# First 1024 tokens started in two token halves, with new loads, conv reads and a split last block

## The chip, the cores and the metric

The kernel runs on one core of one Trainium2 chip. The metric is device time in microseconds (us) of one execution, as the median of several runs. The core's engines run side by side, each in the order of its own program, and wait for each other through semaphores: TensorE (PE in the profile; PEld is its weight load), VectorE (DVE), ScalarE (ACT), GpSimd (POOL), and SyncE (SP), which here only issues DMAs. ACT and POOL issue DMAs as well.

## The reference

```python
def _attn_ref(x, weight):              # x (8, 4096, 192), weight (8, 7)
    w = softmax(weight, axis=-1)       # one set of 7 taps for each of 8 heads
    x_pad = concat([zeros(8, 6, 192), x], axis=1)
    # head h owns channels 24h .. 24h+23
    out[b, s, h, :] = sum_k w[h, k] * x_pad[b, s + k, h, :]
def _moe_ref(x, w_in, w_out):          # w_in (192, 2048), w_out (2048, 192)
    h = x @ w_in
    g = where(h > 0, h, exp(min(h, 0)) - 1)
    return g @ w_out
```

The softmax is written short here; the reference subtracts the maximum and adds 1e-9 to the sum. 32768 tokens go through a causal 7-tap convolution along the sequence and then through the two products with an ELU between.

## The kernel before, in words

**Tiling.** The tokens are cut into 32 "supers" of 1024 tokens; a super is two groups g (or r) of 512. The feed-forward width of 2048 is cut into 16 slices q of 128. A step n is one pair (super, q). In each step each group has one unit: three matmuls "h" (L993) of 64 rows by 512 tokens, one for each third j of the 192 channels, which sum into one PSUM bank. Group 0 uses rows 0 to 63 of the array and group 1 rows 64 to 127, so two streams of matmuls run side by side; the code calls a stream `rt`. w_in lies in both row halves.

**ELU.** Each unit goes through three engines: ACT takes exp out of PSUM into E (L739), POOL clamps it to at most 1 (L692), DVE writes gT = max(E - 1, h) as fp16 (L855). Only then is the unit's PSUM bank free. There are eight banks.

**Second product.** Matmuls "o" (L1016) take gT of 128 tokens and w_out of one q into an accumulator for (k, g), where k counts half supers of 256 tokens per group. Each accumulator is evacuated (L746, the last one by DVE at L846) and sent out (L544).

**Convolution.** For supers 1 to 31 it is a product with a band matrix `Tm` ("c", L968): windows of 112 tokens, stationary 64 (and 54) rows by 112 columns, 240 moving columns of xg, 16 matmuls a super. ACT evacuates into csb (L735) and a transposing DMA puts it into `att`. `Tm` is made through a band written to DRAM and read back (L1039, L1048). The channels are split as 24h + 8j + e, so a read of one third j of a head takes 8 neighbouring elements at a time.

**The first super** has no such time, and is done another way: x is loaded whole by ACT's queue (L704), cast in three pieces (L714), transposed on PE (L916; L927 for the 8 tokens ahead of group 1), evacuated (L811 on DVE, L726 on ACT), convolved on PE with seven diagonal matrices `taps` (made by one instruction, L791), and evacuated into `att` (L730, L838, L840). Of thirds 0 and 1, two of the seven taps are computed on DVE (L820, L825: `ON_DVE`). Before this, PE runs ten matmuls on zeros (L890, `WARM`), six ahead of the broadcast of the softmaxed taps (L894, L901) and four after it.

**What sets the order.** A planner in plain Python writes the order of every engine before the launch. `live` plays the first 16 steps against a small model of the engines (durations such as `MM_H`, `MM_O`, `MM_C` and expected landings `LANDS`), `block_items` and `emit` the rest; the result is sorted by time into `pe_order`, `act_order` and `dve_order`. At run time each engine follows its list and waits.

**DMA queues.** POOL issues, in this order: w_in in three column parts of three DMAs each (L628), the first of three parts of w_out (L639), x of super 1 (two DMAs, L608), the other parts of w_out, x of super 2; then it begins with the clamps. w_in lands in rows 0 to 63; its copy for rows 64 to 127 is made by ACT (L720), DVE (L843) and a DMA of SP (L1056).

Of the kernel before, what the change touches and what calls it, by code (L numbers as in the profile page):

```python
# [37 lines left out]
WARM = (6, 1, 4)  # L38
WCOLS = ((0, 4 * FC), (4 * FC, 8 * FC), (8 * FC, 16 * FC))
WOUT = (0, 4, 8, 16)  # L40
HALO = 8
BW = P
ON_DVE = (2, 2, 0)
XL = GS - CW * (NWIN - 1) + PAD
XI = SUP // P
# [7 lines left out]
LATE_Q, COPY_AT = 10, 6  # L53
LIVE, UNTIL = 16, 16
EARLY_O = (4, 8)
LANDS = {"x": {1: 7200.0, 2: 14200.0}, "w_in": 10200.0, "w_out": (3900.0, 8400.0, 11000.0)}
# [3 lines left out]
TURNS = 260.0  # L60
X_AT = ((2, 1, 1), (1, 1, 0))
ZERO_AT = 8
# [3 lines left out]
def bass_lightweight_conv__then__act_elu_kernel(  # L66
# [21 lines left out]
    NK = 2 * NS  # L88
# [12 lines left out]
    conv_half = {}  # L101

# [15 lines left out]
    def modelled():  # L118
        return step[0] < UNTIL
# [9 lines left out]

    def h_items(n, r):  # L130
        def issue(j):
            take_bank(("h", n, r), r)
            plan.append((clock[r], ("h", n, r, j)))
            if j == 2:
                freed[bank_of["h", n, r]] = clock[r] + MM_H + HELD["h"]
                if modelled():
                    elu(n, r, clock[r] + MM_H)

        return [(MM_H, lambda j=j: issue(j), None) for j in range(3)]
# [15 lines left out]
    def o_items(k, g, rt, qs, visit, first, final):  # L155


        todo = [(q, kb) for q in qs for kb in range(2)]

        def issue(i):  # L160
            q, kb = todo[i]
            take_bank(("a", k, g), rt)
            if modelled():
                t = NQ * (k // 2) + q
                clock[rt] = max(clock[rt], gt_at[t, g], turned.get((k, g), 0.0) if first and i == 0 else 0.0)
            starts, ends = first and i == 0, final and i == len(todo) - 1
            item = ("o", k, g, rt, q, kb, visit if starts else None, ends)
            plan.append((clock[rt] - AHEAD, item))
            if ends:
                visits[k, g] = visit + 1  # L170
                turned[k, g] = clock[rt] + MM_O + TURNS
# [36 lines left out]
    def block_items(n, g, rt):  # L208
        k, b = divmod(n - O_AT[g], NB)
        if k < 1:  # L210
            q = n - EARLY_O[g]
            if not 0 <= q < NQ:
                return []
            items = o_items(0, g, rt, range(q, q + 1), 2 * q + rt, True, True)
            return evacuated(items, 0, g) if q == NQ - 1 and rt == 1 else items
# [3 lines left out]
    def live(last, convs, turns):  # L219
        hq = [list(range(last)) for _ in range(2)]  # L220
        cq = [list(convs), list(convs)]
        far = float("inf")

        def h_ready(rt):
# [8 lines left out]
            late = rt == 1 and s == 0 and q >= LATE_Q  # L233
            return max(min(freed), att_at[s], LANDS["w_in"] if late else 0.0)
# [11 lines left out]
        def o_ready(rt, g):  # L246
# [5 lines left out]
            t = max(gt_at.get((NQ * (k // 2) + q, g), far) for q in range(q0, q1))  # L252
# [6 lines left out]
        while any(hq) or any(cq) or any(map(any, turns)):  # L259
            best = None  # L260
            for rt in range(2):
# [22 lines left out]
            if what[0] == "h":  # L284
                n = hq[rt].pop(0)
                go(h_items(n, rt))
            elif what[0] == "c":
# [7 lines left out]
            else:  # L295
                g = what[1]
                k, q0, q1, visit = turns[rt][g].pop(0)
                go(o_items(k, g, rt, range(q0, q1), visit, True, True))
# [9 lines left out]
    start_up = [("t", j) for j in (0, 3, 1, 2)] + [("d", j) for j in range(3)]  # L308
    for i, (b, what) in enumerate(
        ((0, ("t", 0)), (3, ("t", 3)), (1, ("t", 1)), (2, ("t", 2)))  # L310
        + ((4, ("d", 0)), (5, ("d", 1)), (6, ("d", 2)), (7, ("d", 2)))
    ):
        occupant[b], freed[b] = what, i - 10.0
        bank_of.setdefault(what, b)
    turns = [[[], []], [[], []]]
    for rt in range(2):
        for g in range(2):
            turns[rt][g] += [(0, q, q + 1, 2 * q + rt) for q in range(LIVE - EARLY_O[g])]
    live(LIVE, [(n, m) for n in range(LIVE) for m in conv_steps.get(n, ())], turns)
    for n in range(LIVE, NP):  # L320
        step[0] = n
        if n == UNTIL:
            clock[:] = [max(clock)] * 2
# [11 lines left out]
    for second in range(2):  # L335
        for rt in range(2):
# [3 lines left out]
            if second == 0:  # L340
                lead = TAIL - (late - QB * b)
                for kk, q0, q1, v, first in (
                    (k, QB * b, late, 2 * b, True),
                    (k + 1, 0, lead, 0, True),
                    (k, late, NQ, 2 * b, False),
                    (k + 1, lead, NQ, 0, False),
                ):
                    tail[rt] += o_items(kk, g, rt, range(q0, q1), v, first, not first)
            else:
                for kk, q0, v in ((k, QB * b, 2 * b), (k + 1, 0, 0)):  # L350
# [4 lines left out]
    pe_order += [("w", 0, WARM[0]), ("s",), ("w", 0, WARM[2])]  # L355
    for what in start_up:
        pe_order.append(what)
# [3 lines left out]
    for at, item in sorted(plan, key=lambda p: p[0]):  # L361
        if item[0] == "h" and item[3] == 2:
# [3 lines left out]
            act_order.append(item[:3])  # L366
        elif item[0] == "c" and item[2:] == (1, HU - 1):
# [18 lines left out]
    x_before = {}  # L386
    for s in range(2, NS):
# [11 lines left out]
    with ExitStack() as stack:  # L399
# [15 lines left out]
        xs = sbuf("xs", [P, XI, D], FP32)  # L415
        xh = sbuf("xh", [HALO, D], FP32)
        xbh = sbuf("xbh", [HALO, 3, 2, HP], BF16)
        xb = sbuf("xb", [P, 3, XI, HP], BF16)
# [16 lines left out]
        part = sbuf("part", [P, 2, GS], FP32)  # L435
# [10 lines left out]
        s_w = [sema(f"s_w{i}") for i in range(6)]  # L446
        s_wc = sema("s_wc")
        s_sel = sema("s_sel")
# [5 lines left out]
        s_xs = sema("s_xs")  # L454
# [17 lines left out]
        s_wd = sema("s_wd")  # L472
        s_wa = sema("s_wa")
        s_band = sema("s_band")
        s_part = sema("s_part")
# [35 lines left out]
        def att_need(s):  # L511
# [4 lines left out]
            ("t", 0): (0, 1),  # L516
            ("t", 1): (1, 0),
            ("t", 2): (2, 0),
            ("t", 3): (0, 2),
            ("d", 0): (0, 3),  # L520
            ("d", 1): (0, 4),
            ("d", 2): (3, 5),
# [7 lines left out]
        def transposed(j):  # L530
            if j == 3:
                return xT[:, :, 0:HALO], H[:, bank_of["t", 3], 0 : 3 * HALO].rearrange(
                    "p (j c) -> p j c", j=3
                )
            return xT[:, j, HALO : HALO + GS], H[:, bank_of["t", j], :]

        def first_att(j, c0, c1):
            b = bank_of["d", j] + (j == 2 and c0 > 0)
            return att[:, 0, j, c0:c1], H[:, b, c0:c1]

        def out_group(eng, k, g):
            t, half = divmod(k, 2)
            row = SUP * t + GS * g + 2 * P * half
            eng.dma_start(  # L544
                out[row : row + 2 * P, :].rearrange("(k p) d -> p k d", p=P),
                osb[:, k % 2, g, :, :],
            ).then_inc(s_out[k % 2], 16)
# [25 lines left out]
        def out_evac(W, k, g):  # L573
            W(s_out[k % 2], 32 * (k // 2))
            W(s_fin[g], k + 1)
            return (
                osb[:, k % 2, g, :, :].rearrange("p k d -> p (k d)"),
                acc_of(k, g)[:, 0 : 2 * D],
# [14 lines left out]
        def _gpsimd(g: bass.BassGpSimd):  # L593
# [31 lines left out]
            def load_w_in(k):  # L625
                c0, c1 = WCOLS[k]
                for j in range(3):
                    g.dma_start(  # L628
                        w_in[0:HP, j, c0:c1],
                        bass.AP(  # L630
                            tensor=moe_w_in.tensor,
                            offset=8 * j * FF + c0,
                            ap=[[CPH * FF, HEADS], [FF, 8], [1, c1 - c0]],
                        ),
                    ).then_inc(s_w[k], 16)

            def load_w_out(k):
# [3 lines left out]
                ).then_inc(s_w[3 + k], 16)  # L641
# [11 lines left out]
            ).then_inc(s_id)  # L653
            for step in range(2):
# [20 lines left out]
            load_w_in(0)  # L675
            load_w_in(1)
            load_w_in(2)
            load_w_out(0)
            for gr in range(2):
                load_x(1, gr)  # L680
            load_w_out(1)
            load_w_out(2)
            for gr in range(2):
                load_x(2, gr)
# [17 lines left out]
        def _scalar(a):  # L702
            W = Waits(a)
            a.dma_start(  # L704
                xs[:, :, :], x_flat[0:SUP, :].rearrange("(p i) d -> p i d", i=XI)
            ).then_inc(s_xs, 16)
# [5 lines left out]
            W(s_xs, 16)  # L712
            for j in range(3):
                a.activation(  # L714
                    xb[:, j, :, :].rearrange("p i (h e) -> p (i h) e", e=8),
                    xs[:, :, :].rearrange("p i (h j e) -> p j (i h) e", j=3, e=8)[:, j],
                    ACT.Copy,
                ).then_inc(s_cast)
            def upper_half(c0, c1):
                a.activation(  # L720
                    w_in[HP:P, :, c0:c1], w_in[0:HP, :, c0:c1], ACT.Copy
                ).then_inc(s_wa)

            for j in range(1, 3):
                W(s_xt, j + 2)
                a.activation(*transposed(j), ACT.Copy).then_inc(s_fa)  # L726
            W(s_w[0], 48)
            upper_half(*WCOLS[0])
            W(s_first, 3)
            a.activation(*first_att(2, 0, GS // 2), ACT.Copy).then_inc(s_fa)  # L730
            for item in act_order:
                if item[0] == "c":
# [3 lines left out]
                elif item[0] == "h":  # L736
# [5 lines left out]
                    if i == COPY_AT:  # L742
                        W(s_w[2], 48)
                        upper_half(WCOLS[2][0], FC * LATE_Q)
# [6 lines left out]
        def _vector(v):  # L751
            W = Waits(v)

# [33 lines left out]
            ).then_inc(s_set)  # L787
            W(s_sel, 1)
            v.tensor_copy(wcol[:], H[:, bank_of["d", 2], 0:KSIZE]).then_inc(s_tap)
            W(s_tap, 1)  # L790
            v.tensor_tensor(  # L791
                taps[:],
                ident[:, :].unsqueeze(1).to_broadcast([P, KSIZE, P]),
                wcol[:, :].unsqueeze(2).to_broadcast([P, KSIZE, P]),
                ALU.mult,
            ).then_inc(s_tap)
            W(s_xh, 16)
            W(s_xz, 1)
            v.tensor_copy(
# [298 lines left out]
```

## Time and profile before

| | us |
|---|---|
| median of 3 runs (723.69 to 724.35) | 723.8 |
| the profiled execution, whole | 723.52 |
| its span in the profile | 721.7 |
| x landed, first cast begins (L714) | 5.45 |
| first conv matmul of super 0 (L944) | 8.09 |
| first h matmul (L993) | 11.68 |
| first exp (L739) / clamp (L692) / gT (L855) | 12.76 / 13.47 / 14.20 |
| last evacuation begins (L846) | 718.31 |

Times in the profile count from the start of the span. In a row of the timeline the first two numbers are start and duration, "x24" is the number of instructions merged into the row, and a name such as "H<-att,w_in" is the output and its inputs (H is PSUM). What follows "<-" in brackets is what ended the engine's idle time. PE's matmuls are pipelined: a duration in a row includes the way through the array, and what one matmul costs in a dense stream is the distance between starts.

### The profile page before, as it was taken

The page shows a single profiled execution, that of the slowest core. Times are in us where ns is not written, and L with a number is a line of the kernel's source. Part 1 is how long each engine was busy: PE and PEld are TensorE (multiplying, and loading weights), DVE is VectorE, ACT ScalarE, POOL GpSimd, SP SyncE. Part 2 cuts the span into 40 slices and gives each one's busy share as a digit, 9 for nine tenths or more (in the row PEclk, how much of TensorE's full clock was granted, in tenths as well). Part 3 has the DMA queues.
Part 4 walks back from the last instruction along what each step waited for, and adds up shares of the span by engine and source line. Part 5 has one row for each costly group of instructions (what it writes and reads, how often), then busy time and mean ns, then how long its engine had stood idle before and what let it go on. Part 6 is the DMA issues. An engine that isn't in the chain of part 4 may idle for free.

```text
span 721.7 us, 27608 instructions
## 1 busy us (share of the span) xinstructions
PE 715.8 (99%) x11846; PEld 677.6 (94%) x11847; DVE 642.7 (89%) x1048; ACT 677.9 (94%) x1287; POOL 670.0 (93%) x1115
## 2 busy tenths in 40 slices
PE   8999999999999999999999999999999999999998
PEld 4689999999999999999999999999999999999997
DVE  7988898998899988989888989988989989999994
ACT  6999999999999999999999999999999999999994
POOL 9999999999999999999999999999999999999893
PEclk9999999999999999999999999999999999999999
DMA  9655353554254663344553555652535543644212
GB/s 171 92 87 75 67 91 74 95 87 82 54 96 72 87 97 61 75 84 85 87 97 50 84 74 96 86 85 51 96 73 90 92 69 66 94 77 83 71 35 68
DMA packets 132703, 58.75 MB, mean 81 GB/s; under 512 B 98582, under 2 KB 132004, under 8 KB 132580
## 3 DMA queue, kind: packets, MB, share of 16 engines
q1 hardware_dynamic: 88228, 39.23, 23.8%
q0 software_dynamic: 43936, 16.77, 22.8%
q8 instruction: 93, 1.52, 0.8%
q10 hardware_dynamic: 416, 0.98, 0.4%
q14 instruction: 30, 0.25, 0.2%
HBM read 34.63 MB, written 25.46 MB: 83 GB/s over the span
## 4 chain that ended last, share of the span: by engine, by line
PE 95%; POOL 2%; DVE 1%; ACT 1%; issue 0%; DVEq 0%; POOLq 0%
PE H L1016 54%; PE H L993 38%; PE H L968 3%; DVE gT L855 1%; POOL w_in L628 1%; ACT E L739 1%; POOL xg L608 0%; POOL w_out L639 0%; ACT csb L735 0%; POOL E L692 0%; POOL owner L656 0%; DVE osb L846 0%; ACT osb L746 0%; POOL block L666 0%; POOL ident L645 0%
## 5 line engine op out<-in xcount | busy, mean ns | idle before, releaser
L855 DVE SCALAR_TENSOR_TENSOR gT<-E,H 128x512 f16<-128x512 f32 x1024 | 632.8, 681 | 65.0 <-POOL E L692 63.2
L1016 PE MATMUL H<-w_out,gT 64*128 64x192 f16 x8192 | 681.9, 243 | 0.1
L993 PE MATMUL H<-att,w_in 64*128 64x512 bf16 x3072 | 680.0, 376 | 0.5 <-DVE gT L855 0.3
L1016 PEld LDWEIGHTS H<-w_out,gT 64*128 64x128 f16 x8192 | 624.0, 94 | 22.9 <-PE H L1016 1.8
L692 POOL TENSOR_SCALAR E<-E 128x512 f32<-128x512 f32 x1024 | 607.6, 614 | 39.3 <-ACT E L739 28.6
L739 ACT ACTIVATE E<-H 128x512 f32<-128x512 f32 x1024 | 592.7, 601 | 27.3 <-PE H L993 1.6
L993 PEld LDWEIGHTS H<-att,w_in 64*128 64x128 bf16 x3072 | 275.4, 93 | 7.8 <-issue 1.2
L968 PE MATMUL H<-xg,Tm 64*112 64x240 bf16 x496 | 92.5, 266 | 0.1
L735 ACT ACTIVATE csb<-H 112x480 bf16<-112x480 f32 x124 | 70.0, 565 | 0.3 <-PE H L968 0.2
L746 ACT ACTIVATE osb<-H 128x384 f32<-128x384 f32 x127 | 61.6, 486 | 7.5 <-PE H L1016 7.4
L968 PEld LDWEIGHTS H<-xg,Tm 64*112 64x112 bf16 x496 | 57.5, 125 | 3.3 <-DVE gT L855 1.1
L608 POOL DMA_DIRECT2D xg<-in_x_dram x62 | 55.3, 893 | 0.2 <-issue 0.2
L846 DVE COPY osb<-H 128x384 f32<-128x384 f32 x1 | 0.6, 556 | 7.3 <-PE H L1016 7.3
L890 PE MATMUL H<-zw 128*128 128x512 bf16 x10 | 4.4, 606 | 1.2 <-DVE zw L754 1.2
L628 POOL DMA_DIRECT2D w_in<-in_moe_w_in_dram x9 | 5.2, 617 | 0.0
L890 PEld LDWEIGHTS H<-zw 128*128 128x128 bf16 x10 | 1.1, 133 | 3.0 <-issue 1.7
L714 ACT ACTIVATE xb<-xs 128x512 bf16<-128x512 f32 x3 | 1.7, 618 | 2.4 <-DMA xs<-in_x_dram 2.4
L944 PE MATMUL H<-xT,taps 128*128 128x256 bf16 (+1 forms) x23 | 3.7, 314 | 0.2 <-issue 0.2
L944 PEld LDWEIGHTS H<-xT,taps 128*128 128x128 bf16 x24 | 2.2, 97 | 1.5
L639 POOL DMA_DIRECT2D w_out<-in_moe_w_out_dram x3 | 2.6, 879 | 0.0
L707 ACT ACT_TABLE_LOAD x1 | 1.3, 1283 | 1.2 <-PEq L1083 1.2
L720 ACT ACTIVATE w_in<-w_in 64x1536 bf16<-64x1536 bf16 (+1 forms) x2 | 2.3, 1162 | 0.0
(43 smaller groups left out, 19.7 us busy)
## 6 DMA issues: line engine op xcount, KB each, us to landing
out_dram<-osb SPq DMA_DIRECT2D x127, 192.0 KB, 3.4
xg<-in_x_dram POOLq DMA_DIRECT2D x61, 240.0 KB, 5.0
xs<-in_x_dram ACTq DMA_DIRECT2D x1, 768.0 KB, 4.6
att<-csb SPq DMA_TRANSPOSE x31, 4.3
w_in<-in_moe_w_in_dram POOLq DMA_DIRECT2D x6, 64.0 KB, 2.9
w_in<-in_moe_w_in_dram POOLq DMA_DIRECT2D x3, 128.0 KB, 5.2
w_out<-in_moe_w_out_dram POOLq DMA_DIRECT2D x2, 192.0 KB, 9.0
w_out<-in_moe_w_out_dram POOLq DMA_DIRECT2D x1, 384.0 KB, 11.7
```

Of the source, the lines that this page charges most:

```text
L608: g.dma_start(xg[0:rows, b, 2 * w0 + gr : 2 * w1 : 2, :], src).then_inc(s_x[b][gr], 16)
L628: g.dma_start(w_in[0:HP, j, c0:c1], bass.AP(tensor=moe_w_in.tensor, offset=8 * j * FF + c0, ap=[[CPH * FF, HEADS], [FF, 8], [1, c1 - c0]], ...
L692: g.tensor_scalar(out=E[:, i % NE, :], in0=E[:, i % NE, :], scalar1=1.0, scalar2=0.0, op0=ALU.min, op1=ALU.max,).then_inc(s_clp)
L735: a.activation(*conv_evac(W, m), ACT.Copy).then_inc(s_ce)
L739: a.activation(E[:, i % NE, :], H[:, bank_of[item], :], ACT.Exp).then_inc(s_exp)
L746: a.activation(*out_evac(W, *item[1:]), ACT.Copy).then_inc(s_oev[item[2]])
L855: v.scalar_tensor_tensor(out=gT[:, s % NG3, q, u, :], in0=E[:, i % NE, :], scalar=1.0, in1=H[:, bank_of[item], :], op0=ALU.subtract, op1=A ...
L890: pe.matmul(H[:, bank, :], zw[:, 0:P], zw[:, 0:GS], start=True, stop=True)
L944: ins = pe.matmul(H[:, bank_of[item] + half, c0:c1], taps[:, tap, :], xT[:, j, HALO - PAD + tap + c0 : HALO - PAD + tap + c1], start=(tap ...
L968: ins = pe.matmul(H[0:CW, bank_of["c", m], 256 * q : 256 * q + UC], Tm[rows, h, 0:CW], xg[rows, s % NXB, :, CPH * h : CPH * (h + 1)].rearr ...
L993: ins = pe.matmul(H[:, bank_of[item[:3]], :], w_in[HP * r : HP * (r + 1), j, FC * q : FC * (q + 1)], att[HP * r : HP * (r + 1), s % 2, j, ...
L1016: ins = pe.matmul(acc_of(k, g)[:, D * kb : D * (kb + 1)], gT[HP * rt : HP * (rt + 1), t % NG3, q, g, t0 : t0 + P], w_out[HP * rt : HP * (r ...
```

## The change

The first super is worked in two halves of 256 tokens per group (`GH` = 256).

- ACT's queue issues the 8 halo tokens (before: SP's) and x in two DMAs, one for each half. The cast is one instruction a half.
- Transposes "t" and convolution "d" of half 0 come first; the transposes "T" of half 1 follow directly. The convolution "D" of half 1 stands in the planner's list: 7 taps of third 0, then of 1, after two steps of h, and of third 2 after three (`JOBS`). All 21 taps run on PE; DVE's part is gone. The evacuations go to ACT (d 0, d 2, D 0 and 1 together, D 2) and DVE (d 1, T).
- The first four steps are two q's each on half 0 (q 0 to 7, six matmuls of 256 columns), the next four the same on half 1 (`SPLIT`). Then steps are whole again.
- `taps` is made by seven instructions; the transposed halo is evacuated among them. Only one matmul on zeros comes after the broadcast, not four.
- w_in is loaded in four DMAs of 512 columns (before: nine), the first ahead of `owner` and `block8` on POOL. The order is then w_in 1 to 3, w_out 0 and 1, x of super 1, w_out 2; x of super 2 is issued ahead of the first clamp, as before.
- The upper rows of w_in are copied by DVE (parts 0 and 1), ACT (q 8 and 9) and SP's DMA.
- Channels are split as 3c + j: conv matmuls read every third element of xg. Their stationary is all 128 columns of `Tm`, not 112.
- The accumulators of the last half super are split into two of 128 tokens, so there is one evacuation and one store more per group, each half as large.

```diff
-WARM = (6, 1, 4)
-WCOLS = ((0, 4 * FC), (4 * FC, 8 * FC), (8 * FC, 16 * FC))
+WARM = (6, 1, 1)
+NCH = 4
+LATE_Q, COPY_AT = 10, 8
+SPLIT = 8
-ON_DVE = (2, 2, 0)
+JOBS = ((2, ("D", 0, 0)), (2, ("D", 0, 1)), (3, ("D", 1, 2)))
-    NK = 2 * NS
+    NK = 2 * NS + 1
...
-    start_up = [("t", j) for j in (0, 3, 1, 2)] + [("d", j) for j in range(3)]
+    start_up = [("t", 3), ("w", 0, WARM[2]), ("t", 0), ("t", 1), ("t", 2)]
+    start_up += [("d", j) for j in range(3)] + [("T", 0), ("T", 1)]
...
+            load_w_in(0)
             for step in range(2):
                 W(s_id, 2 + step)
...
-            load_w_in(0)
             load_w_in(1)
             load_w_in(2)
+            load_w_in(3)
             load_w_out(0)
+            load_w_out(1)
             for gr in range(2):
                 load_x(1, gr)
-            load_w_out(1)
             load_w_out(2)
-            for gr in range(2):
-                load_x(2, gr)
...
-            a.dma_start(
-                xs[:, :, :], x_flat[0:SUP, :].rearrange("(p i) d -> p i d", i=XI)
-            ).then_inc(s_xs, 16)
+            a.dma_start(xh[:, :], x_flat[GS - HALO : GS, :]).then_inc(s_xh, 16)
+            for half in range(2):
+                a.dma_start(
+                    xs[:, XI * half : XI * (half + 1), :].rearrange("p i d -> p (i d)"),
...
+            cast(0)
             for j in range(3):
                 W(s_xt, j + 2)
+                a.activation(*first_evac(("t", j)), ACT.Copy).then_inc(s_fa)
+            cast(1)
+            for j in (0, 2):
+                W(s_first, j + 1)
+                a.activation(*first_evac(("d", j)), ACT.Copy).then_inc(s_fa)
...
+            for tap in range(KSIZE):
+                if tap == 1:
+                    W(s_xt, 1)
+                    v.tensor_copy(*first_evac(("t", 3))).then_inc(s_fd)
+                v.tensor_scalar(
+                    out=taps[:, tap, :],
...
+            upper_half(0)
+            W(s_first, 2)
+            v.tensor_copy(*first_evac(("d", 1))).then_inc(s_fd)
             for j in range(2):
+                W(s_xt, 5 + j)
+                v.tensor_copy(*first_evac(("T", j))).then_inc(s_fd)
+            upper_half(1)
...
-                        H[0:CW, bank_of["c", m], 256 * q : 256 * q + UC],
-                        Tm[rows, h, 0:CW],
+                        H[:, bank_of["c", m], 256 * q : 256 * q + UC],
+                        Tm[rows, h, :],
                         xg[rows, s % NXB, :, CPH * h : CPH * (h + 1)].rearrange(
-                            "p w (j i) -> p j w i", j=3
+                            "p w (i j) -> p j w i", j=3
                         ),
```

## The prediction

> **What bounds the kernel now.** I read the shares of the page first, then the chain that ended last, then the timeline of the first 30 us and of the last 7, then single groups. On the page PE is busy all the time, but three others are close behind:
>
> ```profile
> PE 715.8 (99%) x11846; PEld 677.6 (94%) x11847; DVE 642.7 (89%) x1048; ACT 677.9 (94%) x1287; POOL 670.0 (93%) x1115
> ```
>
> The chain tells them apart by stage (start, duration, what):
>
> ```profile
> 2.48 0.73 POOL w_in L628
> 3.22 4.43 POOL w_in L628 x8
> 7.65 0.80 POOL w_out L639
> ...
> 13.51 0.67 POOL E L692
> 14.20 0.70 DVE gT L855
> 15.03 1.92 PE H L993 x9
> ...
> 27.91 6.67 DVE gT L855 x11
> ...
> 64.81 0.25 PE H L993 x2
> ...
> 86.67 0.25 PE H L993 x2
> ```
>
> The reader is to see three stages. Up to 13.5 us a queue of DMA issues on POOL and, beside it, the first super's convolution. Then ELU: DVE alone gives 11 units in 6.67 us, 0.606 us a unit. From about 44 us the same PE rows return every 86.67 - 64.81 = 21.86 us, one super. With the planner's costs, which the starts of the timeline bear out, a stream of PE has 48 h x 0.216 + 128 o x 0.0825 + 8 c x 0.1025 = 21.75 us a super. So the middle is PE, with 0.11 us a super to spare, or 3.1 us over 28 supers.
>
> How much start-up is lost: PE's work over the whole kernel is 1536 x 0.216 + 4096 x 0.0825 + 248 x 0.1025 = 695.1 us a stream. It ends at about 718.2 and begins at 11.68. So 718.2 - 11.7 - 695.1 - 3.1 = 8.3 us are idle after the first h, before 44 us, while units wait for ELU. In that stage PE is not the bound; when ELU starts and how fast it runs sets the time at which PE becomes dense, and all that follows moves with it.
>
> ```profile
> 1.22 1.28 ACT L707 ACT_TABLE_LOAD   x1 [1.22 <-PEq L1083]
> 4.39 1.69 PE L890 MATMUL H<-zw 128*128 128x512 bf16 x4
> 5.45 1.67 ACT L714 ACTIVATE xb<-xs 128x512 bf16<-128x512 f32 x3 [2.40 <-DMA xs<-in_x_dram]
> 8.09 3.65 PE L944 MATMUL H<-xT,taps 128*128 128x512 bf16 x23 [0.16 <-issue]
> 12.76 3.54 ACT L739 ACTIVATE E<-H 128x512 f32<-128x512 f32 x7 [0.60 <-PE H L993]
> 14.20 11.07 DVE L855 SCALAR_TENSOR_TENSOR gT<-E,H 128x512 f16<-128x512 f32 x18 [1.03 <-POOL E L692]
> ```
>
> To be seen in these timeline rows: x is waited for until 5.45; the convolution takes 3.65 us for 10 x 512 + 14 x 256 = 8704 columns, 0.42 ns each; ACT needs 3.54/7 = 0.51 us a unit and DVE 11.07/18 = 0.615, so DVE is the slower once it runs.
>
> **The change, part 1: when ELU starts.** *Taps.* ACT issues three DMAs ahead of its table load, not one: 0.28 (the halo's issue, as it was on SP) + 0.39 = 0.67 us later. The exp of the taps, the small DVE chain and the broadcast move with it: taps' column at 4.49 + 0.67 = 5.16. The halo cast (0.34) fits ahead of it while PE works. Seven tap instructions cost at least the one of now (1.09); with the halo's evacuation (0.17) and a little for each they end at about 6.7, and the band's cast (0.19) at 6.9, before 6.1. *x.* The whole x took 4.6 us from issue to landing. A half is issued at 1.08 and lands between 1.08 + 2.3 = 3.4 and 5.7; I take 4.2. Its cast, 768 elements at the 0.52 us of 512, is 0.8, so done at 5.0. That is hidden: on PE the halo's transpose and one zero matmul (1.69/4 = 0.42) come first, until 5.8. *PE.* 24 transposes at the pace of the 48 now (some 0.03 each) end at 6.6, ACT evacuates the first from 6.25 (0.38, L730's shape) to 6.65. Then 21 matmuls x 256 columns x 0.42 = 2.26 us, so 6.75 to 9.0, then T, 24 x 0.03 = 0.7: the first h at 9.7, against 11.68. Its third j needs the evacuation of d 2, 9.0 + 0.2 + 0.38 = 9.6. ACT's cast of half 1 (0.8) lies behind the evacuations, 7.3 to 8.1, and hides under the convolution. Six h of 0.108 us: the first exp at about 10.6, against 12.76, 2.15 us earlier.
>
> *POOL* must keep up. Nine w_in issues (0.73 + 4.43 = 5.2 us) become four. Bounds: 4 x 0.58 = 2.3 and 4 x 0.9 = 3.6 (issues of xg and w_out, with more pieces each); I take 0.65 each, 2.6. The queue that ends at 13.5 now ends at 10.9, just ahead of the first clamp at 11.2. At 0.9 each it would hold the clamp until 11.9 and cost 0.7. Moving the first w_in ahead delays `block8` to 3.2 us, which is used at 4.6: nothing. *DVE* has its pre-work (two copies of w_in at 0.93, three evacuations) done at 11.6, and starts gT at about 12.1, against 14.20.
>
> **Part 2: what is given back.** The convolution of half 1 costs PE 21 x 0.108 = 2.3 us between steps. It hides in the 8.3 idle us; without them it would cost 2.3. But its evacuations stand in ACT's list between exps: 0.49 + 0.38 = 0.85. DVE is slower than ACT by 0.1 a unit, so part could hide; yet the copy of w_in (0.84, L720) and four evacuations of the next super (0.57 each) follow on ACT within the next units. So of 2.15 I count 0.85 and 0.1 of gaps off: **1.2 us gained**; bounds 2.1 (all hidden) and 0.4 (POOL's 0.7 also lost).
>
> The w_in and w_out loads start up to 2 us earlier on POOL, but the DMA engines are full (in the first 25 us the shares of the 16 engines stand at 8 and 9 tenths), so they land less early, and the band goes out 0.8 later. What is late next is `Tm`, now 8.0 us from issue to landing at about 19.2: PE would stand at super 1's first conv (now at 20.5) for up to 1 us. DVE has some 3 us of units in banks then; cost 0, at worst 1.
>
> **Part 3: the clock of PE.** Six matmuls on zeros take 2.74 us, 0.83 ns a column, and the four later ones run at the same pace; only the convolution runs at 0.42. So PE is at half rate until between 5.6 and 8.1, and the four zero matmuls fill PE from 4.4 to 6.1. The change leaves one, so PE is nearly idle from 3.8 to 5.0. If full rate then came only at about 9.2, some 11 of the 21 matmuls would take 0.213 and not 0.108: 1.15 us. I take nothing, since PE is busy before and after the hole; bounds 0 and 1.15. [...]
>
> **Part 4: the conv of the other 31 supers.**
>
> ```profile
> L968 PEld LDWEIGHTS H<-xg,Tm x40: 122/127/129, 204.0 to 253.9; 64*112 64x112 bf16 x20, 54*112 54x112 bf16 x20
> ```
>
> A load of 112 columns takes 127 ns, one of 128 columns 94 (L1016). The wider one should take 94: 33 ns less, 16 times a super, beside running matmuls; only a load behind a wait is in the open. Bounds: 0, and the whole 0.11 us a super, 3.1. One exposed load a super is 0.9; as a different start can also shift the planned order I take **0.5 us gained**, with -1 at the other end.
>
> The moving read takes every third element, not 8 neighbours. No row shows that. The nearest is the conv itself, whose read jumps after each 8 elements and yet costs 0.1025 us for 240 columns, the same 0.42 ns as a plain row: cost 0. A gain is excluded, as that is already the plain rate. The far end is two reads' time per column, as where PE's transposes write PSUM with a stride (64 columns at some 53 ns, not 27): 0.1 x 248 = 25 us. I take 0, the row being the same instruction. [...]
>
> **Part 5: the tail.**
>
> ```profile
> 718.31 0.56 DVE L846 COPY osb<-H 128x384 f32<-128x384 f32 x1 [7.29 <-PE H L1016]
> 718.90 0.40 ACTq L544 DMA_DIRECT2D out_dram<-osb  x1
> ```
>
> The last evacuation halves. Between 128x256 (0.424, L840) and 128x24 (0.172, L811) a column costs 1.1 ns, so 192 columns less save 0.2. The last store, 2.8 us from issue to the end of the span, carries half the bytes: between 0 and 0.3, I take 0.2. **0.4 us gained.** The added evacuation and store lie earlier, beside PE's last 16 matmuls per stream.
>
> **Sum.** 1.2 + 0.5 + 0.4 = 2.1 us. The profiled execution took 723.52 (span 721.7 and 1.8 around it), so 721.4; the median lies 0.3 above that execution, so **721.7**.
>
> **Rivals.**
> - *Half-rate PE* through the convolution (part 3): 721.7 + 1.15 = 722.9. For it, the hole; against it, busy stretches on both sides. 0.17.
> - *Data come too late*: ELU starts early, but w_out, w_in's upper rows or `Tm` land no earlier, and PE, in order, stands before them. DMA shares near full speak for it, the banks of units ahead of DVE against it. 1.2 us lost: 722.9. This is also the case that the change doesn't do what it says. 0.16.
> - *Slower: the strided conv read.* Place: L968, 248 matmuls a stream. From 2.1/25.4 = 8% per conv matmul on, all gain is gone; at twice the time 721.7 + 25 = 747. For it, that no row shows such a read; against it, the conv row of now. 0.11.
> - Forecast: 0.56.
>
> **How the numbers follow.** About 0.2% (1.45 us, so 722.35 and 725.25) is what can be told from no change. The bounds, taken together, run from 723.8 - (2.1 + 2.0 + 0.5) = 719.2, where part 4 is not counted whole, since its 3.1 would need every idle ns of the middle to be a weight load, to 723.8 - (0.4 - 1 + 0.2) = 724.2. The forecast is faster 8 times in 10, the two cases at 722.9 three in ten: 0.45 + 0.10 = 0.55. Slower: the strided read, and 0.06 from late data with a worse order: 0.17. Same: 0.28. The range goes from 719.2 to 724.5: it takes in these bounds and both cases at 722.9 with their spread, and leaves out the strided read.
>
> **What would show it.** First h near 9.7, first exp near 10.6, first gT near 12.1; D's evacuations between exps; starts of the convolution's matmuls 0.108 apart (0.213: the clock). Dense PE rows from 43 us on, and repeating every 21.84 to 21.86 (22.6 for the strided read). Last evacuation 0.35. Wrong would be: gT starting early, but DVE idle between units by as much; or the period longer.

## The result, and the profile after

The changed kernel takes **760.4 us** (median of 4 runs, 759.84 to 761.15), beside 724.08 for the kernel before on the same chip: 1.050 times as long (95% interval 1.0486 to 1.0518). The forecast of 721.7, with a range of 719.2 to 724.5, was wrong. The profiled execution took 760.21 with a span of 758.3; before it was 721.7, so 36.6 us have to be found. (Two single executions further down, of 1928 and 1065 us where the others of their kernels took 738 to 740 and 723 to 726, are left out of the numbers.)

First the page of the changed kernel, busy time by engine. PE's busy time grew by 16.8 us though it does nearly the same work:

```profile
PE 732.6 (97%) x11910; PEld 677.9 (89%) x11910; DVE 646.4 (85%) x1050; ACT 680.8 (90%) x1291; POOL 669.3 (88%) x1110
```

Then the chain that ended last, in order of time (start, duration, what):

```profile
2.10 27.97 DMA xs<-in_x_dram
30.10 0.85 ACT xb L775
30.99 1.49 PE H L980 x24
32.48 2.67 PE H L1064 x24
...
224.96 0.30 PE H L1064 x2
...
247.26 0.30 PE H L1064 x2
...
269.56 0.30 PE H L1064 x2
...
755.73 0.36 DVE osb L888
```

Two things are to be seen. The chain now begins with a load of x that ends at 30.07; the load of the whole x had ended at 5.45. And the same PE rows return every 22.30 us, no longer every 21.86.

The timeline of the changed kernel's first 40 us shows both halves waited for, and the clock besides:

```profile
1.43 1.19 ACTq L759 DMA_DIRECT2D xs<-in_x_dram  x2
17.71 0.84 ACT L775 ACTIVATE xb<-xs 128x768 bf16<-128x768 f32 x1 [13.23 <-DMA xs<-in_x_dram]
20.03 3.79 PE L1003 MATMUL H<-xT,taps 128*128 128x256 bf16 x21
30.10 0.84 ACT L775 ACTIVATE xb<-xs 128x768 bf16<-128x768 f32 x1 [9.57 <-DMA xs<-in_x_dram]
32.41 2.74 PE L1064 MATMUL H<-att,w_in 64*128 64x256 bf16 x24
35.25 2.55 DVE L904 SCALAR_TENSOR_TENSOR gT<-E,H 128x512 f16<-128x512 f32 x4 [1.41 <-POOL E L745]
```

Half 0 landed at 17.7, 13 us after ACT stood ready for it. The order of PE's list puts T, the transposes of half 1, before the first h, so the first h waits for half 1 as well: 32.41, where it was 11.68. Two windows of that stage (length, busy us of PE, PEld, DVE, ACT and POOL, then granted clock, DMA share, GB/s) show that PE's clock fell too, while PE had little to do:

```profile
17.70:30.10 12.40, 5.21 (x45) 3.88 (x45) 0.43 (x1) 2.00 (x5) 0.00 (x0) 0.84 0.53 111
30.10:32.50 2.40, 1.51 (x26) 1.34 (x28) 0.40 (x1) 1.39 (x3) 0.00 (x0) 0.50 0.20 24
```

Last, the matmuls of the conv in the middle (min/median/max ns), first in the kernel before, then their row and that of their weight loads in the changed kernel:

```profile
L968 PE MATMUL H<-xg,Tm x40: 260/263/307, 204.1 to 254.0; 64*112 64x240 bf16 x20, 54*112 54x240 bf16 x20
```

```profile
L1028 PE MATMUL H<-xg,Tm x45: 325/328/333, 199.8 to 259.9; 64*128 64x240 bf16 x23, 54*128 54x240 bf16 x22
L1028 PEld LDWEIGHTS H<-xg,Tm x44: 92/93/94, 200.3 to 259.7; 54*128 54x128 bf16 x22, 64*128 64x128 bf16 x22
```

The median went from 263 to 328 ns, and two of one stream that follow each other began 0.102 to 0.107 us apart before (one in eight up to 0.147); now 0.162 to 0.170. The weight load did fall from 127 to 93 ns, as forecast. So there are two suspects: **20.7 us** until the first h, and 0.44 us a super, **some 13 to 14 us** over 31 supers. From the start of the last evacuation to the end of the span it is 2.57 us, 0.8 less than before.

### The profile page after: what moved, and what is told of

Same layout as the page of the kernel before. It is cut to its first block, busy times and chain, and to the rows that moved or that the text cites. A ratio compares the mean times of both kernels' runs of the same rounds, so it can differ in the third digit from the quotient of the medians.

```text
span 758.3 us, 27738 instructions
## 1 busy us (share of the span) xinstructions
PE 732.6 (97%) x11910; PEld 677.9 (89%) x11910; DVE 646.4 (85%) x1050; ACT 680.8 (90%) x1291; POOL 669.3 (88%) x1110
## 4 chain that ended last, share of the span: by engine, by line
PE 94%; DMA 4%; ACT 1%; DVE 0%; POOL 0%; ACTq 0%; issue 0%; DVEq 0%
PE H L1087 51%; PE H L1064 38%; PE H L1028 5%; DMA xs<-in_x_dram 4%; PE H L1003 0%; DVE gT L904 0%; ACT E L797 0%; PE H L980 0%; POOL E L745 0%; ACT csb L793 0%; ACT xb L775 0%; ACT w_in L803 0%; ACTq L759 0%; ACTq L757 0%; DVE osb L888 0%
## 5 line engine op out<-in xcount | busy, mean ns | idle before, releaser
L904 DVE SCALAR_TENSOR_TENSOR gT<-E,H 128x512 f16<-128x512 f32 x1024 | 639.2, 683 | 75.4 <-POOL E L745 73.3
L1064 PE MATMUL H<-att,w_in 64*128 64x512 bf16 (+1 forms) x3120 | 681.2, 374 | 0.2 <-ACT csb L793 0.2
L1064 PEld LDWEIGHTS H<-att,w_in 64*128 64x128 bf16 x3120 | 280.3, 94 | 5.1 <-DVE gT L904 1.0
L1028 PE MATMUL H<-xg,Tm 64*128 64x240 bf16 x496 | 122.6, 329 | 0.5 <-DVE gT L904 0.2
L807 ACT ACTIVATE osb<-H 128x384 f32<-128x384 f32 (+1 forms) x129 | 62.1, 483 | 6.8 <-PE H L1087 6.8
L1028 PEld LDWEIGHTS H<-xg,Tm 64*128 64x128 bf16 x496 | 42.1, 93 | 6.1 <-PE H L1028 1.4
L980 PE MATMUL H<-ident,xb 64*64 64x64 bf16 x48 | 3.0, 342 | 19.3 <-ACT xb L775 19.3
L881 DVE CAST att<-H 128x256 bf16<-128x256 f32 x1 | 0.4, 426 | 14.1 <-PE H L1003 14.1
L1003 PE MATMUL H<-xT,taps 128*128 128x256 bf16 x42 | 7.1, 338 | 0.0
## 6 DMA issues: line engine op xcount, KB each, us to landing
w_out<-in_moe_w_out_dram POOLq DMA_DIRECT2D x1, 384.0 KB, 26.2
```

The lines of the kernel that those rows point to most:

```text
L807: a.activation(*out_evac(W, *item[1:]), ACT.Copy).then_inc(s_oev[item[2]])
L904: v.scalar_tensor_tensor(out=to, in0=e, scalar=1.0, in1=h, op0=ALU.subtract, op1=ALU.max,).then_inc(s_tt)
L980: ins = pe.matmul(H[rows, bank_of[item], c0 + i : c0 + GH : XI], xb[rows, XI * half + i, j::3], ident[rows, rows], start=(i == 0 and j == ...
L1003: ins = pe.matmul(H[:, bank_of[item[:2]], p0 : p0 + GH], taps[:, tap, :], xT[:, j, c0 + tap : c0 + tap + GH], start=(tap == 0 and (not hal ...
L1028: ins = pe.matmul(H[:, bank_of["c", m], 256 * q : 256 * q + UC], Tm[rows, h, :], xg[rows, s % NXB, :, CPH * h : CPH * (h + 1)].rearrange(" ...
L1064: ins = pe.matmul(H[:, bank_of[item[:3]], c0 : c0 + t1 - t0], w_in[HP * r : HP * (r + 1), j, FC * q : FC * (q + 1)], att[HP * r : HP * (r ...
```

## The experiments

**Theory A: the loads of a half run on 2 of 16 DMA engines.** The source of each half is written `[[GS*D, 2], [XI*D, HP], [1, XI*D]]`: its first dimension is 2. In the trace the semaphore of half 0 got one update at 2.48 us, just after the issue, and then only two, at 17.49 and 17.69, when data landed; that of the old load got sixteen, at 4.22 to 5.43. The loads of weights beside it got sixteen each, of which the last two came late: for the fourth part of w_in fourteen by 10.70 and two at 17.02 and 17.31, for the second of w_out fourteen by 13.76 and two at 29.60 and 29.99. To take each landing for one engine, and the first dimension for the cause, is the author's reading; the runs test what follows from it. **Theory B: the conv's read of every third element is slower on PE.** Its rival: the stationary of 128 columns is.

*Each half in two loads of 64 rows, one for each group (code shortened):*

```diff
-    a.dma_start(xs[:, half], AP(ap=[[GS * D, 2], [XI * D, HP], [1, XI * D]]))
+    for g, queue in ((0, a), (1, sy)):
+        queue.dma_start(xs[HP*g : HP*(g+1), half], AP(ap=[[XI * D, HP], [1, XI * D]]))
```

> The kernel after, with each half of x loaded by two DMAs, one per group of 512 tokens (64 rows of 3 KB each; group 0 on ACT's queue, group 1 on SP's), so that no pattern begins with a dimension of 2. Theory A (a load whose source begins with a dimension of 2 runs on 2 of the 16 DMA engines): both halves land by about 6 us, the first h comes at 10 to 12 us and not at 32.4, and the time falls by about 21 us, to 737 to 742 us. Rival (the halves starve behind the w_in and w_out loads, which POOL now issues earlier): half 0 lands later than 12 us and the time stays above 752 us.

739.07 us (three executions), 21.3 less than the changed kernel: theory A. The profile is of the execution left out and shows nothing of the others.

*The kernel before, with its one load of x written as 2 x 64 rows:*

> The kernel before, with its one load of x written with a source of 2 x 64 rows and not 128; the same bytes go to the same places in the same queue. Theory A: x lands at 25 to 31 us and not at 5.4, and the time rises by 18 to 25 us, to 742 to 749 us. Rival (it is the cut into halves or the early w_in load that delays x): no change, 724 us.

724.11, ratio 0.9999 (0.9989 to 1.0009). This told nothing: the two dimensions lie one behind the other, and 16 landings were counted, as with the 128 rows of the kernel before; the author took them to be joined again. The next run mends it.

*The same with 8 tokens left out between the two, so that they can't be joined (code shortened):*

```diff
-    x_flat[0:SUP, :].rearrange("(p i) d -> p i d", i=XI)
+    AP(ap=[[(GS + 8) * D, 2], [XI * D, HP], [1, XI * D]])
```

> The kernel before, with its one load of x written as 2 x 64 rows where the second 64 rows begin 8 tokens later, so that the two dimensions can't be joined into 128 rows (the first super's second group then holds tokens 520 to 1031: its output is not the reference's). The run e2 was joined into 128 rows again and so tested nothing. Theory A: x lands at 25 to 31 us and not at 5.4, on 2 engines, and the time rises by 18 to 25 us, to 742 to 749 us. Rival (the halves or the earlier loads delay x): 724 us.

745.36, +21.5 (ratio 1.0296, 1.0277 to 1.0315). The cast's row of this run:

```profile
24.75 1.67 ACT L719 ACTIVATE xb<-xs 128x512 bf16<-128x512 f32 x3 [20.96 <-DMA xs<-in_x_dram]
```

The same bytes, in the kernel before, by one number in the pattern: 24.75 in place of 5.45, with two landings and not sixteen.

*The changed kernel with all of POOL's loads behind both halves of x* (are two engines slow, or is it that weights share them?):

```diff
+            for half in range(2):
+                W(s_xs[half], 16)
             load_w_in(0)
```

> The kernel after, but POOL issues its first load of w_in, and all behind it, only when both halves of x have landed, so that the halves have the DMA engines to themselves. Theory A (2 engines, 64 rows of 3 KB each per engine and half, some 0.13 us a row): half 0 lands at about 11 us and half 1 at about 19, later than the whole x of the kernel before in spite of the free engines. Rival (starved by the other loads): half 0 lands by 5 us, half 1 by 6.5.

755.14 (one execution). The row of its first cast:

```profile
11.86 0.84 ACT L777 ACTIVATE xb<-xs 128x768 bf16<-128x768 f32 x1 [7.37 <-DMA xs<-in_x_dram]
```

Half 0 landed at 11.8 and half 1 at 19.6: so a half of 393 KB takes about 8 to 10 us with nothing large beside it. A row of 3 KB took 0.124 us in this run (median), and 64 of them one after the other on each of two engines would make 7.9 us, an estimate from that row. The rest of 17.7 and 30.1, 5.9 and 10.5 us, came with the weights beside them. That cut both ways: in the changed kernel the weights were late as well (the fourth part of w_in landed at 17.3 and the second of w_out at 30.0; with the loads repaired, further down, at 12.4 and 15.1).

*The conv of the changed kernel reads runs of 8 again* (channel order of the kernel before, in this read alone):

```diff
-    "p w (i j) -> p j w i", j=3
+    "p w (j i) -> p j w i", j=3
```

> The kernel after, but the conv matmuls of supers 1 to 31 read 8 neighbouring elements at a time, as before, and not every third (so each third of a head holds other channels than w_in's rows: the output is not the reference's). Theory B (the strided read costs 0.0575 us more per conv matmul): the starts of two conv matmuls in one stream are 0.1025 us apart again and not 0.160, a super takes 21.8 us and not 22.3, and the time falls by 0.0575 x 248 = 14.3 us, to about 746 us. Rival (the 128 wide stationary or the planned order costs it): 760 us.

747.17, 13.2 less. *The kernel before with the read of every third element* (the same line, `(j i)` to `(i j)`):

> The kernel before, but its conv matmuls read every third element (the output is not the reference's: each third of a head holds other channels), with the stationary still 112 wide. Theory B: 724.1 + 14.3 = 738 us, and 22.3 us a super. Rival (the read is free and the 128 wide stationary costs): 724 us.

738.16, 14.1 more (ratio 1.0192, 1.0176 to 1.0207). The conv rows of these two runs, first the changed kernel with runs of 8, then the kernel before with every third:

```profile
L1028 PE MATMUL H<-xg,Tm x44: 260/263/273, 200.3 to 256.9; 64*128 64x240 bf16 x22, 54*128 54x240 bf16 x22
```

```profile
L968 PE MATMUL H<-xg,Tm x44: 325/329/367, 201.5 to 259.3; 64*112 64x240 bf16 x22, 54*112 54x240 bf16 x22
```

The time follows the read and not the width, in both kernels. The expected 0.0575 us x 248 are 14.3 us a stream; 13.2 and 14.1 were measured, 53 and 57 ns a matmul.

*Width alone, in the kernel before:*

```diff
-                        H[0:CW, bank_of["c", m], 256 * q : 256 * q + UC],
-                        Tm[rows, h, 0:CW],
+                        H[:, bank_of["c", m], 256 * q : 256 * q + UC],
+                        Tm[rows, h, :],
```

> The kernel before with 128 columns of the band as stationary and not 112, its read in runs of 8. By the forecast's part 4: a weight load of 94 ns and not 127, and 0.5 us less (0 to 3.1): 723.6 us. Rival (no load was in the open, or the order shifts): 724.1 us and more.

723.29 beside 723.85: ratio 0.9995 (0.9986 to 1.0004), not to be told from nothing. The traces tell more, one execution each. From the start of the 36th gT to that of the last, this run needs 673.3 us; four with 112 columns (the kernel before, the two with x's pattern rewritten, and the one with fewer zero matmuls below) need 673.9 to 674.05, and all six with 128 columns and runs of 8 need 673.2 to 673.4. So the wide stationary is worth some 0.65 us in the middle. Its place is seen too: between 200 and 600 us, which is 18 supers, the kernel before has 18 conv matmuls with 64 rows that start 146 or 147 ns after their neighbour, and here those 18 start 112 or 113 ns after it: one load a super was in the open, and it is 34 ns shorter.

*Both repairs, the four loads of x and the runs of 8, in the changed kernel (the two diffs above together):*

> The kernel after with both repairs: x in four loads of 64 rows, and conv reads in runs of 8 (output not the reference's, as in e3). If A and B are all of the loss and add up: 760.4 - 21 - 13.2 = 726 us. If the rest of the change is worth what was forecast: 721.7 us. If A and B overlap: above 728 us.

724.87, ratio 1.0014 (1.0005 to 1.0024) to the kernel before. So of the 36.3 us lost A and B are all but 1.0. But the forecast's gain isn't there either. Rows of this run:

```profile
2.79 1.28 ACT L770 ACT_TABLE_LOAD   x1 [2.79 <-issue]
6.54 0.84 ACT L778 ACTIVATE xb<-xs 128x768 bf16<-128x768 f32 x1 [1.92 <-DMA xs<-in_x_dram]
8.38 3.95 PE L1006 MATMUL H<-xT,taps 128*128 128x256 bf16 x21
13.06 1.48 PE L1067 MATMUL H<-att,w_in 64*128 64x256 bf16 x24
```

x lands at 6.5 (forecast 4.2), the conv takes 3.95 (2.26), the first h is at 13.06 (9.7). The granted clock stood at 0.5 from 8.03 to 11.45 (the next two texts on record put such times 0.3 us too early), and the conv's matmuls start 0.213 us apart until 11.34 and 0.11 from 11.51 on. Over the conv the granted clock was 0.61 on average (first row below, columns as above); in the last repaired version further down, whose conv takes 2.48 us, it was 1.00 (second row):

```profile
8.38:12.30 3.92, 3.92 (x25) 2.71 (x25) 0.96 (x2) 1.72 (x4) 2.63 (x4) 0.61 1.22 170
```

```profile
8.06:10.50 2.44, 2.44 (x23) 1.98 (x23) 1.47 (x4) 1.50 (x4) 2.44 (x4) 1.00 1.00 109
```

Three runs try these causes, and a fourth the tail; for all four the kernel before took 724.07. In the first text, "weights read in runs of 8" is a slip for the conv's read of x; as in the run above, in it and in the last repaired version that read takes other channels than the reference's.

*Both repairs, and four more zero matmuls ahead of the broadcast:*

```diff
-WARM = (6, 1, 1)
+WARM = (10, 1, 1)
```

> The kernel with both repairs (four loads of x, weights read in runs of 8; 724.9 us) with four more zero matmuls ahead of the tap matmuls, so that TensorE works from 1.25 to 5.67 where it had stood from 3.99 to 5.67. Nothing else changes. Theory C, the clock: TensorE's granted clock fell to 0.5 from 7.7 to 11.1 in the repaired kernel because of that hole, so the 21 matmuls of the first conv took 3.95 us in place of about 2.3. Filled, the clock stays 1.0, the first conv takes 2.3 to 2.6 us, the first h comes at 11.4 to 11.8 in place of 13.06, and the time is 723.3 to 724.0 us (1.5 less at the start, part of it lost again to what comes next: w_in's copies, DVE's evacuations of half 1). Rival, the conv of half 0 is slow by its shape: first conv 3.9 us still, first h at 13.0, time 724.9.

723.76, ratio 1.0003 (0.9994 to 1.0012). Its executions fall in two groups: seven at 723.4 to 723.8 and four at 725.0 to 725.6. The profiled one is of the second, its clock was at 0.5 from 8.13 to 11.54, and its conv took 3.75 us, so filling the hole didn't always keep the clock. The ratio is 0.0011 lower than without them, and the two intervals overlap. That the half clock slows the conv is carried by its record, by the starts of the matmuls, which change their distance where the record changes, and by the conv at 2.48 us under a clock of 1.0. Here and in the last repaired version the five executions with a mean clock of 0.998 took 725.3 to 725.6 and the others 723.4 to 725.0; with the repairs alone the mean clock doesn't part them. That the hole makes the clock fall isn't shown: it fell here without the long one.

*The kernel before with one zero matmul after the broadcast, not four:*

```diff
-WARM = (6, 1, 4)
+WARM = (6, 1, 1)
```

> The kernel before with one zero matmul after the tap matmuls in place of four, so that TensorE stands from about 4.9 to 6.1. Theory C, the clock: if a hole of 1.2 us is enough, the granted clock falls to 0.5 somewhere between 7.7 and 11.1, the 23 matmuls of the first conv take 5 to 7 us in place of 3.65 and the time rises by 1 to 2.5 us to 724.9 to 726.4. Rival, a hole as short as this does nothing (the repaired kernel had one of 1.7 us and another of 0.85): conv 3.65, time 723.9 within 0.3.

Median 724.91, ratio 1.0005 (0.9995 to 1.0015): inconclusive. Six of 11 executions lie at 724.9 or above, against 7 of 35 of the kernel before. The clock's record began at 1.0 only at 10.3 here (5.75 in the kernel before) and the conv took 4.5 us. But the run with the wide stationary, which starts as the kernel before does, had it at 10.5 and 725.02 in its profiled execution. So the start of full clock varied from 5.75 to 10.5 with the same start of the kernel; a hole may make the late case more frequent, and no more is shown.

*Both repairs, zero matmuls, and x ahead of the first weight load (code shortened):*

```diff
-            load_w_in(0)
             for step in range(2):
...
+            W(s_xs[0], 32)
+            load_w_in(0)
             load_w_in(1)
...
-            a.dma_start(xh[:, :], x_flat[GS - HALO : GS, :])
+            sy.dma_start(xh[:, :], x_flat[GS - HALO : GS, :])   # after x
```

> The kernel with both repairs and the four zero matmuls, and two moves: GpSimd issues its first weight load only after half 0 of x has landed, and the load of the 8 halo rows goes out from SP behind x, so that ACT's table load comes 0.6 us sooner. Theory D, in the repaired kernel half 0 of x lands at 6.5 because the first weight load shares the DMA engines with it: it lands at 4.5 to 5.2, the cast starts 1.3 to 2 us sooner, the first conv at 7.0 to 7.4 (the taps then set it), the first h at 10 to 10.6, and the time is 721.9 to 723.0. The forecast's start (first h 9.7) is then all but reached. Rival, the weights then come late: the second q of w_in waits for its load and its copy, the first units fall apart, and the time is that of the kernel with zero matmuls alone or above it (723.5 to 725).

724.16, ratio 1.0002 (0.9993 to 1.0011). Theory D is right about x and wrong about the time. (Of the 1.9 us that x lands earlier, some 0.6 may be ACT's issue, now at 0.80 and not 1.43, since the halo's goes behind it.) Rows of its timeline:

```profile
4.64 0.84 ACT L778 ACTIVATE xb<-xs 128x768 bf16<-128x768 f32 x1 [0.79 <-DMA xs<-in_x_dram]
8.06 2.48 PE L1006 MATMUL H<-xT,taps 128*128 128x256 bf16 x21
11.28 1.48 PE L1067 MATMUL H<-att,w_in 64*128 64x256 bf16 x24
11.77 1.72 POOL L673 DMA_DIRECT2D xg<-in_x_dram  x2
12.14 2.06 ACT L800 ACTIVATE E<-H 128x512 f32<-128x512 f32 x4 [1.18 <-PE H L1067]
13.52 3.54 POOL L756 TENSOR_SCALAR E<-E 128x512 f32<-128x512 f32 x6
14.18 3.68 DVE L907 SCALAR_TENSOR_TENSOR gT<-E,H 128x512 f16<-128x512 f32 x6 [1.03 <-POOL E L756]
14.44 0.60 ACT L792 ACTIVATE att<-H 128x512 bf16<-128x512 f32 x1 [0.23 <-PE H L1006]
```

Here x lands at 4.6 and the conv takes 2.48, as the forecast wanted. The first exp is 0.6 earlier than before (12.14 against 12.76), yet the first gT isn't (14.18 against 14.20): POOL, whose loads wait for x here, issues them until 13.49 and clamps only then. Then D's evacuations stand between the exps (L792: 0.60, and 0.39 at 16.16), and ACT waits for PE five times around them, 0.15 to 0.31 us each: from unit 5 to unit 12 DVE needs 5.8 us, before 4.3. This is read from the rows; no run takes the evacuations away. So the kernel is 1.5 us behind the one before at unit 36, 0.7 behind at the last unit (the wide stationary), and equal after the shorter tail.

*The split last block and the wide stationary alone, in the kernel before (code shortened):*

```diff
-    NK = 2 * NS
+    NK = 2 * NS + 1      # and blocks_of(k), as in the changed kernel
...
-                for kk, q0, v in ((k, QB * b, 2 * b), (k + 1, 0, 0)):
+                for kk, q0, v in ((k, QB * b, 2 * b), (k + 1, 0, 0), (k + 2, 0, 0)):
...
-                        Tm[rows, h, 0:CW],
+                        Tm[rows, h, :],
```

> The kernel before with two parts of the change alone: the last output block of each group is taken out in two quarters with stores of their own, and the stationary of the conv is 128 columns wide. Theory T, the tail's gain is real and stands by itself: the last evacuation takes 0.36 us in place of 0.50, the stretch from its start to the end of the span falls from 3.36 to about 2.6 us, and the time is 723.0 to 723.3 (0.8 less with 0 to 0.3 for the width). Rival, the tail's gain in the changed kernel came from its late start alone (the outputs were due in another order): time 723.9 within 0.3.

**723.13**, ratio 0.9984 (0.9975 to 0.9993), the lowest median of all: a gain of 0.9 us. Its last rows, however, are not those expected:

```profile
715.18 3.54 SPq L551 DMA_DIRECT2D out_dram<-osb  x5
717.38 0.36 DVE L854 COPY osb<-H 128x192 f32<-128x192 f32 x1 [7.29 <-PE H L1024]
717.77 0.36 ACTq L551 DMA_DIRECT2D out_dram<-osb  x1
```

The evacuation did shrink to 0.36, but the end of the span comes 3.32 us after its start, not 2.6: one of SP's five stores took 1.43 us to issue and held the next two. The last gT began 0.9 earlier than before, at 709.4: 0.2 at unit 36 already and 0.7 from there on, as in the other runs with the wide stationary. So in this execution the gain was made before the tail, and theory T's price for the tail isn't shown here. From the start of the last gT to the end it takes 11.27 us here, 11.34 to 12.04 in six traces without the split, and 10.57 to 10.60 in six of the changed kernel and its repairs, so there the tail is 0.7 us shorter or more, also where it doesn't begin late; that the split alone does it isn't shown. How the two parts share the 0.9 of the median stays open.

## Why the prediction was wrong

- **What bounds the kernel** was read rightly: PE in the middle, the start of ELU before. What was added to either showed in the time (21.5 and 14.1 us in the kernel before).
- **Part 1 failed at "A half is issued at 1.08 and lands between 1.08 + 2.3 = 3.4 and 5.7; I take 4.2".** It landed at 17.7, and half 1 at 30.1. The bounds took the pace of the old load (4.6 us from issue to landing) for granted; the pattern itself was not looked at. This is 21.3 of the 36.3 us, and no rival held it: "data come too late" spoke of weights, at 1.2 us. With the loads repaired it lands at 6.5, and with w_in put behind x and x issued 0.6 earlier at 4.6: a DMA moved ahead was counted for POOL's time and not for x's landing.
- *ACT's issues* were priced at 0.28 + 0.39 ahead of the table load. They took 0.59 and 1.19 for two; with the repaired loads the table load came at 2.79, not 1.9.
- *POOL's queue* was forecast well: four w_in issues took 2.7 us (2.6 forecast) and the queue ended at 11.0 (10.9). It held the clamp only in the last repaired version, where it begins at 4.9 behind x and ends at 13.5, as in the kernel before.
- **Part 2**: two evacuations of D between exps were counted at 0.85 (0.49 + 0.38 is 0.87). They took 0.99, and with ACT's waits for PE around them DVE lost 1.5 from unit 5 to 12. The place was right, and the term was too small.
- **Part 3, half-rate PE**, was taken at nothing. In the repaired kernel it came: 3.95 us for 21 matmuls where 2.26 was forecast, 1.7 us, above the bound of 1.15. The rival had 0.17. No run shows the 9.2 us at which the forecast let full rate begin for that bound: it was the author's assumption, and the 1.15 rests on it. What the runs showed is a record at 0.5 from 8.03 to 11.45 with both repairs and from 8.13 to 11.54 with the zero matmuls as well; what sets these times isn't shown.
- **Part 4 failed at "I take 0, the row being the same instruction"** for the strided read. It costs 53 to 57 ns a matmul, 0.44 us a super, 13 to 14 us. The rival on the other side had its place and its cause, the strided read, right, and its far end (25) was about twice the price; it was put at 0.11. That end was an estimate from the transposes (64 columns start 52 to 56 ns apart in the kernel before); that their strided write is the reason isn't shown, nor is why the strided read is slower. Measured are 0.162 to 0.170 us against 0.102 to 0.107 for 240 columns. The same opcode and shape were taken as the same instruction, though its address pattern was what the change altered.
- *The wide stationary*: the load fell to 93 ns as said, and one load a super was in the open. A gain of 0.5 us was taken; the median fell by 0.6, inside the noise, and the traces show 0.65 in the middle.
- **Part 5** had the right sign: 0.4 was forecast, and in the changed kernel 0.8 measured, since the end of the store came sooner as well (2.2 us from issue to the end, before 2.8).

## What to carry to other kernels

When a DMA is rewritten, read the dimensions of its pattern as compiled, not only its bytes, and count in the trace how many landings its semaphore gets: here the pattern with two and not sixteen made the load of x five times as long (24.0 us from issue to cast in the kernel before, where it had been 4.6), and the weights beside such loads were late (17.3 for 12.4, 30.0 for 15.1). When a matmul's moving read gets a stride, price it by a run of that read alone: here the row of the same shape was read as a cost of 0, and 53 to 57 ns a matmul were measured. And a head start at the beginning was worth only what the next engine in line could take: in the last repaired version here the first exp came 0.6 us earlier, and POOL's issues and ACT's evacuations took it all back.

## What the runs showed of the hardware that was not expected

- A load of 393 KB in a pattern that begins with 2 took 8 to 10 us with nothing large beside it, and 28 beside weight loads and behind a first such load.
- PE's moving read of bf16 with a step of 6 bytes took about 1.6 times the time of runs of 8 (0.162 to 0.170 against 0.102 to 0.107 us for 240 columns).
- The granted clock stood at 0.5 from 26.2 to 36.4 while and after PE waited for x, and from about 8.1 to 11.5 in two kernels with shorter holes. In three kernels with the same start its record at 1.0 begins at 4.5, 5.75 and 10.5.
- The issue of one store on SP took 1.43 us where its neighbours took 0.37 to 0.47.
